# Attention stretches and the row of DMAs around the first token blocks: pairs 3 to 6 in fused stretches, with loads, casts and transposing DMAs queued earlier

## The chip, the cores and the metric

One core of one Trainium2 chip. The time of a kernel is the device time of one execution in microseconds (us); medians below are over the executions of one call on one chip. Every ratio is the mean time of one kernel's fast executions over the mean of the other's fast executions of the same rounds, with a 95% interval, so it is not quite the ratio of the medians that stand beside it. Below 1 is faster than the kernel before. "Span" is the time from the first to the last instruction of one profiled execution; it is about 1.7 us shorter than the device time.

## The reference

```python
def _attn_ref(q, k, v):                       # q, k, v: 8 x 8 x 576 x 64
    scores = scale * np.matmul(q, k.transpose(0, 1, 3, 2))
    gamma = 1.0 - 2.0 ** (-5.0 - np.arange(H, dtype=np.float32))
    Dmat = np.where(rel >= 0, gamma[:, None, None] ** rel[None, :, :], 0.0)
    return np.matmul(scores * Dmat[None], v)

def _moe_ref(x, w_a, w_b, w_out):             # x: 4608 x 512, d_ff = 1536
    return ((x @ w_a) * (x @ w_b)) @ w_out
```

A decaying (retention) attention feeds a bilinear feed-forward layer. The kernel works through the tokens in blocks. Blocks 1 and 2 have 256 tokens each, block 3 and the following ones 512. Attention is done for "pairs" of 128-token groups, one or more blocks ahead of the feed-forward work that consumes them.

## The kernel before

Each pair n goes through these stages:

- its q, k and v are loaded in fp32 by DMAs issued on SyncE (two DMAs of 256 KB per tensor);
- GpSimd (POOL) casts and scales them to bf16;
- two transposing DMAs, again on SyncE, turn q and k into qkT;
- a "half stretch" of TensorE (PE) matmuls takes the pair in: kv products for the running state, and sc, the scores, which read qkT;
- another takes it out: o from the states and from the masked scores.

A stretch may be fused: pair n in and pair n-1 out, four sets of 32 small matmuls in a row.

In the feed-forward work pa and pb are the products of x with w_a and w_b. ScalarE (ACT) copies pa to ha, VectorE (DVE) multiplies ha and pb into hT, and po is the output product, which is copied to osb and stored. In the kernel before, pa, pb and kv share the four result buffers (in PSUM) of the pool ps_ffn. The additions of kv to the running state are called "sums", and xT is the finished x of a block.

```python
    def load_pair(n):
        paired[n] = []
        for name, src in (("qf", q), ("kf", k), ("vf", v)):
            t = stage.tile([128, 2 * DM], FP32, tag=name, name=name + "2")
            for kp, r0, m, b, s0 in rows_of(n):
                nc.sync.dma_start(t[r0:r0 + m, kp * DM:(kp + 1) * DM] ..., src[...])
            paired[n].append(t)

    def turn(n):                       # the transposing DMAs, in SyncE's row too
        for w in (0, 1):
            nc.sync.dma_start_transpose(qkT[:, w]..., qkb[:, w])

    def keyed(n):                      # kv of a pair; banks of pa/pb ("ab")
        kvs = [ps_ffn.tile([128, 2, HP, 64], FP32, tag="ab", name=f"kv{a}")
               for a in (0, 1)]
        # ... 32 matmuls, then four additions on VectorE, in one piece:
        later.append(lambda: [add(i) for i in range(4)])

    def stretch(into, outof):
        flush()
        if outof is not None:
            # ... o2 tile, from_states(outof), fence copy on ScalarE
        if into is not None:
            convert, convert_swapped = keyed(into)
            masked = matched(into)     # sc <- qkT: needs the transposes landed
        if outof is not None:
            scaled = from_keys(outof, o, begun)     # o <- sT, vb
            later.append(lambda: scaled(0)); later.append(lambda: scaled(1))
        # ...

    # positions are in units of 512-column matmuls of the feed-forward work
    nc.sync.dma_start(gate, wo_sb[0:1, 3, 0:64])    # waits for output weights
    # ... loads of the last opening steps, then:
    for n in (FIRST, FIRST + 1):       # FIRST = 3
        load_pair(n)
    todo += [(178, stretch, (3, None)), (204, stretch, (None, 3)),
             (228, stretch, (4, None)), (250, stretch, (5, 4)),
             (280, stretch, (None, 5)), (304, stretch, (6, None)),
             (372, stretch, (7, 6)), (408, stretch, (8, 7))]
    casts = {3: 140, 4: 159, 5: 192, 6: 246, 7: 281, 8: 330}
    turns = {4: 196, 5: 222, 6: 258, 7: 338, 8: 345}
    loads = {5: 130, 6: 223, 7: 258.1, 8: 281.1, 9: 345.1, 10: 345.2}
```

The functions in `later` run one at a time between the feed-forward products. The tiny "gate" transfer waits for output weights to land, and SyncE's loads stand behind it, so it decides when the whole row of loads begins (in the profile before, SyncE waited 23.2 us at it for those weights, issued it at 33.45 us and the first load behind it at 34.15 us).

## Time and profile before

| what | number | where from |
|---|---|---|
| time | 333.99 us, median of 3 (333.43 to 334.01) | timing |
| span, PE busy | 332.2 us, 98% | profile |
| first matmul of blocks 1, 2, 3, 4 | 54.12, 73.43, 94.46, 129.00 us | PE timeline |
| gate transfer starts | 33.45 us | SyncE timeline |
| pair 4's transposes issued / used by PE | 67.0 and 69.2 us / 76.4 us | SyncE and PE timelines |

How to read the timelines below: start, duration, engine, line of the kernel, operation, output<-inputs, shape and how many in the group. A bracket at the end gives idle time just before the group, and what ended it.

### The profile page before, as it was taken

To read this page: it belongs to the slowest core of one execution; us is meant where nothing else is said; L and a number is where in the kernel's file an instruction comes from. 1 tells how busy PE (TensorE), PEld (TensorE's weight loads), DVE (VectorE), ACT (ScalarE), POOL (GpSimd) and SP (SyncE) were. 2 spreads that over 40 slices of the span, in tenths; PEclk is the share of its full clock that TensorE was granted. 3 is DMA by queue.
4 is the path that set the end of the run, shared out by engine and by line. 5 is a ranking of instruction groups with operands and counts; after the bars stand their busy time and mean duration, and the time that the engine had idled before them with its cause. 6 is when DMAs were issued, how large, how long until landed. Compare 5 with 4: busy or idle time off the path is not lost.

```text
span 332.2 us, 8708 instructions
## 1 busy us (share of the span) xinstructions
PE 324.9 (98%) x3648; PEld 167.7 (50%) x3648; DVE 163.6 (49%) x292; ACT 128.3 (39%) x275; POOL 114.8 (35%) x146
## 2 busy tenths in 40 slices
PE   8999999999999999999999999999999999999996
PEld 4754457857644554545454545454445444444443
DVE  5744435556646465656266625662456246414321
ACT  7734834445415344353135323532332333213321
POOL 3860078550747377446054404360430000000000
PEclk9999999999999999999999999999999999999999
DMA  7999999989999999994599257955760420031013
GB/s 212 249 186 208 259 228 231 204 163 163 176 226 235 216 201 237 230 202 95 136 229 217 51 132 176 220 87 147 170 128 4 136 56 0 2 95 34 1 26 100
DMA packets 143175, 50.37 MB, mean 152 GB/s; under 512 B 124576, under 2 KB 138656, under 8 KB 143136
## 3 DMA queue, kind: packets, MB, share of 16 engines
q1 hardware_dynamic: 138384, 45.10, 65.6%
q0 software_dynamic: 4752, 4.72, 8.8%
q8 instruction: 28, 0.46, 0.6%
q14 instruction: 11, 0.09, 0.1%
HBM read 37.75 MB, written 9.44 MB: 142 GB/s over the span
## 4 chain that ended last, share of the span: by engine, by line
PE 93%; DVE 2%; DMA 2%; ACT 1%; issue 1%; SPq 0%; POOL 0%; ACTq 0%; DVEq 0%; POOLq 0%
PE po L709 28%; PE pb L689 27%; PE pa L674 27%; PE o L594 2%; DMA qf<-in_q_dram 2%; PE o L581 2%; PE sc L555 1%; PE kv L500 1%; DVE sums L520 1%; PE kv L357 1%; PE tp L314 1%; PE sc L329 1%; PE o L407 1%; PE w L733 0%; SPq L151 0%
## 5 line engine op out<-in xcount | busy, mean ns | idle before, releaser
L694 DVE TENSOR_TENSOR hT<-ha,pb 128x512 bf16<-128x512 bf16 (+1 forms) x120 | 75.7, 633 | 97.6 <-PE pb L689 89.0
L682 ACT CAST ha<-pa 128x512 bf16<-128x512 f32 (+1 forms) x120 | 64.7, 542 | 126.5 <-PE pa L674 125.8
L689 PE MATMUL pb<-xT,wb_sb 128*128 128x512 bf16 (+1 forms) x480 | 111.9, 358 | 0.4 <-DVE sums L520 0.2
L674 PE MATMUL pa<-xT,wa_sb 128*128 128x512 bf16 (+1 forms) x474 | 110.3, 358 | 0.6 <-ACT ha L682 0.4
L709 PE MATMUL po<-wo_sb,hT 128*128 128x512 bf16 (+1 forms) x444 | 97.5, 374 | 0.0
L689 PEld LDWEIGHTS <-wb_sb 128*128 128x128 bf16 x480 | 46.5, 98 | 47.4 <-DVE sums L520 1.2
L674 PEld LDWEIGHTS <-wa_sb 128*128 128x128 bf16 x474 | 45.3, 98 | 46.4 <-issue 1.3
L709 PEld LDWEIGHTS <-hT 128*128 128x128 bf16 x444 | 42.2, 98 | 46.9
L438 POOL CAST qkb<-qf 64x1024 bf16<-64x1024 f32 x15 | 15.5, 1031 | 87.3 <-DMA qf<-in_q_dram 66.7
L720 DVE COPY osb<-po 128x512 f32<-128x512 f32 (+1 forms) x18 | 12.2, 676 | 41.7 <-PE po L709 41.7
L443 POOL TENSOR_TENSOR vb<-vf,vs 128x1024 bf16<-128x1024 f32 x15 | 28.5, 1902 | 11.4 <-DMA vf<-in_v_dram 4.6
L718 ACT COPY osb<-po 128x512 f32<-128x512 f32 (+1 forms) x19 | 10.9, 574 | 43.5 <-PE po L709 43.5
L604 DVE TENSOR_TENSOR xT<-o,qs 128x512 bf16<-128x512 f32 x30 | 19.5, 682 | 6.4 <-PE o L594 6.4
L520 DVE TENSOR_TENSOR sums<-kv,sums 128x256 f32<-128x256 f32 x46 | 19.5, 423 | 2.8 <-PE kv L500 0.8
L564 DVE TENSOR_TENSOR sT<-sc,mask 128x512 bf16<-128x512 f32 x30 | 19.5, 679 | 0.0
L442 POOL CAST qkb<-kf 64x512 bf16<-64x512 f32 x30 | 17.6, 615 | 0.8
L442 POOL CAST qkb<-qf 64x512 bf16<-64x512 f32 x30 | 17.6, 616 | 0.6
L438 POOL CAST qkb<-kf 64x1024 bf16<-64x1024 f32 x15 | 15.5, 1036 | 5.4 <-DMA kf<-in_k_dram 4.6
L524 ACT CAST states<-sums 64x512 bf16<-64x512 f32 x26 | 16.0, 617 | 0.3
L733 PE MATMUL w<-ones 128*128 128x256 bf16 (+1 forms) x36 | 8.5, 367 | 1.5 <-DVE ones L195 1.5
L297 POOL CAST qkb<-kf 128x512 bf16<-128x512 f32 x5 | 3.1, 615 | 18.9 <-DMA kf<-in_k_dram 18.9
L337 DVE TENSOR_TENSOR sT<-sc,mask_s 128x1024 bf16<-128x1024 f32 x6 | 7.3, 1221 | 2.1 <-PE sc L329 2.1
(81 smaller groups left out, 155.2 us busy)
## 6 DMA issues: line engine op xcount, KB each, us to landing
qf<-in_q_dram SPq DMA_DIRECT2D x32, 256.0 KB, 4.2
kf<-in_k_dram SPq DMA_DIRECT2D x32, 256.0 KB, 5.0
vf<-in_v_dram SPq DMA_DIRECT2D x32, 256.0 KB, 5.3
out_dram<-osb SPq DMA_DIRECT2D x25, 256.0 KB, 2.2
out_dram<-osb SPq DMA_DIRECT2D x22, 128.0 KB, 2.4
wo_sb<-in_moe_w_out_dram POOLq DMA_DIRECT2D x3, 512.0 KB, 16.7
qf<-in_q_dram SPq DMA_DIRECT2D x8, 128.0 KB, 3.3
kf<-in_k_dram SPq DMA_DIRECT2D x8, 128.0 KB, 3.4
```

The source lines that it names most:

```text
L438: nc.gpsimd.tensor_copy(qkb[0:64, w], t[0:64])
L442: nc.gpsimd.tensor_copy(to[:, :, 1 - r], fro[:, :, r])
L443: nc.gpsimd.tensor_tensor(vb.rearrange("p (k h d) -> p k h d", k=2, h=H), vf.rearrange("p (k h d) -> p k h d", k=2, h=H), vs2[:, 2 if n in ...
L520: nc.vector.tensor_tensor(sums[:, i], own, prev, op=ALU.add)
L524: nc.scalar.copy(to(half(1 - r)), fro(half(r)))
L564: nc.vector.tensor_tensor(sT[:, on].rearrange("p c k s -> p (c k) s"), sc[:, on].rearrange("p c k s -> p (c k) s"), mask3.unsqueeze(1).to_ ...
L604: nc.vector.tensor_tensor(x_of(t0, 128).rearrange("p c (a s) -> p c a s", a=2), o[:, :, :, kp].rearrange("p a c s -> p c a s"), qs[:, :, s ...
L674: nc.tensor.matmul(pa[:, 0:n], wa_sb[:, c, fs], xT[:, c], start=(c == 0), stop=(c == NC - 1))
L682: nc.scalar.copy(ha[:, 0:n], pa[:, 0:n])
L689: nc.tensor.matmul(pb[:, 0:n], wb_sb[:, c, fs], xT[:, c], start=(c == 0), stop=(c == NC - 1))
L694: nc.vector.tensor_tensor(hT[:, F, 0:n], has[F][:, 0:n], pb[:, 0:n], op=ALU.mult)
L709: nc.tensor.matmul(po[:, 0:width], hT[:, F, u * 128:(u + 1) * 128], wo_sb[:, F, cols], start=(F == 0), stop=(F == NF - 1))
```

## The change

The intent: fewer separate stretches, so that PE switches less often between attention and feed-forward work; VectorE's additions placed where they hold up no product; and pairs 4 to 6 prepared early enough to be taken in sooner.

```diff
+    SPLIT = (3, 5)
-    def load_pair(n):
+    def load_pair(n, which=(0, 1, 2)):
...
-    def keyed(n):
+    def keyed(n, alone):
-        kvs = [ps_ffn.tile([128, 2, HP, 64], FP32, tag="ab", name=f"kv{a}")
-               for a in (0, 1)]
+        if alone:
+            kv = ps_o[0].tile([128, 2, 2, HP, 64], FP32, tag="o", name="kv")
+            kvs = [kv[:, a] for a in (0, 1)]
+        else:
+            kvs = [ps_ffn.tile(... as before ...) for a in (0, 1)]
...
-        later.append(lambda: [add(i) for i in range(4)])
+        parts = [(0, 1), (2, 3)] if n in SPLIT else [(0, 1, 2, 3)]
+        for part in parts:
+            later.append(lambda part=part: [add(i) for i in part])
...
-    for n in (FIRST, FIRST + 1):
+    for n in range(FIRST, FIRST + 3):
         load_pair(n)
...
-    todo += [(178, stretch, (3, None)), (204, stretch, (None, 3)),
-             (228, stretch, (4, None)), (250, stretch, (5, 4)),
-             (280, stretch, (None, 5)), (304, stretch, (6, None)),
+    todo += [(170, stretch, (3, None)), (197, stretch, (4, 3)),
+             (246, stretch, (5, 4)), (280, stretch, (6, 5)),
              (372, stretch, (7, 6)), (408, stretch, (8, 7))]
...
-    casts = {3: 140, 4: 159, 5: 192, 6: 246, 7: 281, 8: 330}
-    turns = {4: 196, 5: 222, 6: 258, 7: 338, 8: 345}
-    loads = {5: 130, 6: 223, 7: 258.1, 8: 281.1, 9: 345.1, 10: 345.2}
+    casts = {3: 104, 4: 104.1, 5: 143, 6: 200, 7: 250, 8: 330}
+    turns = {4: 104.2, 5: 151, 6: 210, 7: 338, 8: 345}
+    loads = {7: 212, 8: 271, 9: 345.1, 10: 345.2}
+    todo += [(150, load_pair, (6, (0, 1))), (152, load_pair, (6, (2,)))]
```

More of the change, by code (lines that the diff above doesn't have):

```diff
@@ L131 @@
     paired = {}
-    def load_pair(n):
+    def load_pair(n, which=(0, 1, 2)):
         if n >= NP:
             return
-        paired[n] = []
-        for name, src in (("qf", q), ("kf", k), ("vf", v)):
+        paired.setdefault(n, [])
+        for i in which:
+            name, src = (("qf", q), ("kf", k), ("vf", v))[i]
             t = stage.tile([128, 2 * DM], FP32, tag=name, name=name + "2")
@@ L491, in keyed @@
         qkb, vb = of(natural, n)
-        kvs = [ps_ffn.tile([128, 2, HP, 64], FP32, tag="ab", name=f"kv{a}")
-               for a in (0, 1)]
+        if alone:
+            kv = ps_o[0].tile([128, 2, 2, HP, 64], FP32, tag="o", name="kv")
+            kvs = [kv[:, a] for a in (0, 1)]
+        else:
+            kvs = [ps_ffn.tile([128, 2, HP, 64], FP32, tag="ab",
+                               name=f"kv{a}") for a in (0, 1)]
         begun = Begun()
@@ L614, in stretch @@
         flush()
+        if into == FIRST:
+            ps_next("ps_pair")
         if outof is not None:
-            if outof == FIRST:
-                ps_next("ps_pair")
             o = ps_o[0].tile([128, 2, HP, 2, 64], FP32, tag="o", name="o2")
@@ L624, in stretch @@
         if into is not None:
-            convert, convert_swapped = keyed(into)
+            convert, convert_swapped = keyed(into, outof is None)
             masked = matched(into)
@@ L699, in ffn_block @@
         for u in range(n // 128):
-            rows = slice(tok0 + u * 128, tok0 + (u + 1) * 128)
-            final = rows.stop == NTOK
+            final = tok0 + (u + 1) * 128 == NTOK
             osb = o_pool.tile([128, DM], FP32, tag="osb", name="osb")
```

## The prediction

> **What bounds the kernel now.** I read the page's busy table and the chain that ended last first, then the waits of the stretch from 54 to 118 us, then the timelines of PE, DVE and SyncE there.
>
> ```profile
> PE 324.9 (98%) x3648; PEld 167.7 (50%) x3648; DVE 163.6 (49%) x292; ACT 128.3 (39%) x275; POOL 114.8 (35%) x146
> ...
> PE 93%; DVE 2%; DMA 2%; ACT 1%; issue 1%; SPq 0%; POOL 0%; ACTq 0%; DVEq 0%; POOLq 0%
> ```
>
> TensorE is busy 98% of 332.2 us and holds 93% of the chain. A change that removes no matmul (here the count stays the same: in the built order only their places differ) can win only what PE loses between matmuls. So I measured this loss where the change works: token blocks 1 and 2 (256 tokens each, 54.12 to 94.46 us) and block 3 (512 tokens, to 117.29 us). The PE timeline shows the pace and the loss:
>
> ```profile
> 62.00 0.60 PE L674 MATMUL pa<-xT,wa_sb 128*128 128x256 bf16 x4
> 62.43 0.60 PE L689 MATMUL pb<-xT,wb_sb 128*128 128x256 bf16 x4
> 62.96 0.45 PE L500 MATMUL kv<-vb,qkb 64*64 64x64 bf16 x32
> 63.24 0.46 PE L555 MATMUL sc<-qkT 64*64 64x64 bf16 x32
> 63.63 0.61 PE L674 MATMUL pa<-xT,wa_sb 128*128 128x256 bf16 x4
> 64.08 0.60 PE L689 MATMUL pb<-xT,wb_sb 128*128 128x256 bf16 x4
> 64.70 0.60 PE L674 MATMUL pa<-xT,wa_sb 128*128 128x256 bf16 x4
> 65.26 0.60 PE L689 MATMUL pb<-xT,wb_sb 128*128 128x256 bf16 x4
> 65.76 0.60 PE L674 MATMUL pa<-xT,wa_sb 128*128 128x256 bf16 x4
> 66.51 0.61 PE L689 MATMUL pb<-xT,wb_sb 128*128 128x256 bf16 x4 [0.16 <-DVE sums L520]
> ```
>
> Starts count here, since matmuls overlap. An undisturbed group of four takes 0.437 us (62.00 to 62.43). After the half stretch of pair 3 (kv and sc) six groups take 3.33 us (63.63 to 66.96) where 2.62 would do: 0.71 us lost with hardly any "idle" shown. The DVE timeline says why:
>
> ```profile
> 64.78 0.42 DVE L694 TENSOR_TENSOR hT<-ha,pb 128x256 bf16<-128x256 bf16 x1 [1.23 <-PE pb L689]
> 65.12 1.79 DVE L520 TENSOR_TENSOR sums<-kv,sums 128x256 f32<-128x256 f32 x4
> 66.83 0.41 DVE L694 TENSOR_TENSOR hT<-ha,pb 128x256 bf16<-128x256 bf16 x1
> 67.16 0.68 DVE L564 TENSOR_TENSOR sT<-sc,mask 128x512 bf16<-128x512 f32 x1
> ```
>
> Four additions hold DVE for 1.79 us, and until they end the two kv tiles keep two of the four PSUM buffers through which pa and pb rotate. PE then waits in turn for ACT (64.70) and DVE (65.26).
>
> [...]
>
> **The change part by part.** First the ideal work of blocks 1 and 2: 48 groups x 0.437 = 20.95 us, 48 output matmuls (L709) x 0.216 = 10.36, four PE transposes sets x 0.22 = 0.88: 32.2 us. The span is 40.34, so 8.1 us are attention work and loss.
>
> Attention before, each from the end of the undisturbed pace to the next big matmul: pair 3 in 0.76; pair 3 out 1.28 (it contains a wait for the fence copy); pair 4 in 0.76; pair 5 in with 4 out 1.37 (83.32 to 84.69); pair 5 out 1.25; sum 5.42. Lost pace: 0.71 + 1.27 + 0.71 = 2.69. Together 8.11, so the account closes. Block 3 adds pair 6 in (0.76) and 7 in with 6 out (1.33), 22.83 us in all, without loss.
>
> After: 3 in; 4 in with 3 out; 5 in with 4 out; 6 in with 5 out; then 7 with 6.
> - Stretches: 0.76 + 3 x 1.36 = 4.84 in blocks 1 and 2 (before 5.42), and block 3 loses its 0.76. Gain 5.42 + 0.76 - 4.84 = 1.34 us. The full stretch is cheap because its four sets of 32 small matmuls follow at 0.27 to 0.3 us and the fence copy hides behind kv and sc.
> - Pair 3's kv moves to the two o banks, which are idle then, and its sums come two at a time between hT products. All four buffers stay in rotation; DVE needs 0.34 + 0.90 us per step of 0.875, so it falls behind by about 0.4 us in each of two steps, within the slack of the freed buffers. Loss 0.71 falls to about 0.1: gain 0.6.
> - Pair 4's half stretch in block 2 goes; its sums now fall in block 1's output phase, where DVE has no hT. Gain 1.27, if the banks come free in time.
> - Pair 5's sums stay in block 2, split in two. But here kv keeps two banks until the second half is done, so pa and pb run on the other two longer: I step it through at 1.13, 1.63, 2.19, 2.80, 3.25, 3.70, 4.13 us after the stretch against 3.50 ideal: loss 0.63 against 0.71. Gain 0.1.
> - Pair 6 in with 5 out stands in block 2's output phase with only 8 output matmuls left (1.73 us) before block 3, whose first matmul reads all of x of pairs 4 and 5. In the built order DVE does four sums, half of x, the copy of the output tile, then the other half of x. Sums can begin about 0.5 us before the stretch ends and take 1.79 (+1.3); half x 0.65 (+1.95); the copy waits for the last output matmul (+1.95 to +2.6); half x to +3.25. Block 3 could begin at +1.73. So PE stands about 1.5 us. Before there were no sums between, and pa followed at once:
>
> ```profile
> 92.72 1.90 PE L709 MATMUL po<-wo_sb,hT 128*128 128x512 bf16 x8
> 94.46 1.03 PE L674 MATMUL pa<-xT,wa_sb 128*128 128x512 bf16 x4
> ```
>
> - Loads, casts, transposes: bytes are unchanged. Pair 5's loads start at about 54.2 instead of 58.5 us and take some 6.4 us, as they do before. The transposes of pair 4 are then issued at about 62.0 and 63.4 us and land 3.8 to 4.6 us later, at 66 to 68. PE reaches sc of pair 4 at about 68.6 us (54.12 + 10.5 + 0.9 + 0.9 + 1.7 + 0.6). The margin is under 1 us; I charge 0.2 us for the chance. Pair 5 lands at about 77 to 78 and is needed at 80.4; pair 6 at about 83.5 and 89. Those are hidden.
>
> ```profile
> 67.02 3.48 SPq L469 DMA_TRANSPOSE qkT<-qkb  x2
> 70.60 4.86 SPq L645 DMA_DIRECT2D out_dram<-osb  x4
> 75.56 3.45 SPq L469 DMA_TRANSPOSE qkT<-qkb  x2
> ```
>
> Here the first pair of transposes waits for its loads' queue and ends at 70.5 against a use at 76.4: the old order has 5 us to spare, the new one spends it.
>
> Sum: 1.34 + 0.6 + 1.27 + 0.1 - 1.5 - 0.2 = 1.6 us; with 334.0 us before that is 332.4. After block 3's output phase the PE order is the same as before and already without waits (117.29 to 129.00 us is all busy), so the gain should reach the end untouched.
>
> **Rivals.**
> - The wait before block 3 is absent or small (the DVE order is less tight than I step it). For: the osb copy takes only 0.69 us, and sums might start earlier. Against: the DVE order is fixed in the program, and in a later stretch of the same form sums and x take 3.07 us together. It would give 330.9.
> - Transposes of pair 4 land late, and PE stands at the sc of that stretch with block 2 behind it. For: DMA is saturated there (1.06 busy share from 54 to 94 us), transposes took up to 5.1 us to land, and the margin is small. It would cost 1 to 2 us: 333.4 to 334.4.
> - DVE falls behind in block 1 and the stretch of 3 in still stalls, and the sums of pair 5 hold banks longer. For: six large DVE operations in five steps. It would cost 0.5 to 1 us: about 333.
> - No gain at all: what is saved before 94 us is waited for afterwards by late casts of pairs 7 and 8. Against: those transposes are not used before block 3's second half, and POOL is idle for 12.5 us waiting for kv before.
>
> **Range and chances.** 332.4, from the sum. All rivals lie between 330.9 and 334.4, and run-to-run spread before is 0.6 us, so 330.7 to 334.0 should hold it 8 times in 10. Two per cent are 6.7 us; blocks 1 and 2 hold only 8.1 us of attention and loss altogether, so neither side is likely: faster 0.02, same 0.96, slower 0.02.
>
> **What would show it.** PE busy must stay near 324.9 us while the span falls. In the PE timeline: two stretches fewer; the pace after pair 3's half stretch near 0.437; an idle of about 1.5 us on PE before block 3's first pa, put down to DVE xT; three or four slow groups after pair 5's stretch. On SyncE, transposes of pair 4 issued at about 62 to 64 us. If the sc of pair 4 shows a wait for a DMA, the second rival holds. If block 3 starts within 0.5 us of its ideal, my reading of the DVE order is wrong. If the time moves by over 4 us, the account of 8.1 us misses something.

## The result and the profile after

The changed kernel took 333.75 us (333.55 to 334.06, 4 executions), the kernel before 333.77 us beside it (333.43 to 334.01, 4 executions): ratio 1.0001 [0.9984, 1.0018]. There is no gain where 1.6 us was forecast. The profiled span is 331.8 us, clock 1.0.

The waits of PE in the changed kernel (waiting for, from whom: total us, times, longest). The lines "issue" of 0.2 us are mostly single matmuls missing from the record (3,612 matmuls are in it beside 3,648 weight loads):

```profile
PE po L716 <- issue: 1.6, 10, 0.2
PE w L740 <- DVE ones L197: 1.5, 1, 1.5
PE pa L682 <- DVE xT L612: 1.4, 1, 1.4
PE sc L563 <- DMA qkT<-qkb: 1.3, 1, 1.3
```

The wait at w is the start of the program and was there before. The other two are new: pa of block 3 waits for VectorE (forecast), and sc waits for transposing DMAs for 1.3 us. The line below answers to the "PE 93%" line of the prediction, with DMA up from 2% to 5%. This is no measure of lost time: 5% of the span is over 16 us, and the chain counts a transfer on it from its issue (pair 4's second transpose stands in it with 4.02 us from 66.07, the moment of its issue). It shows only that the last chain now runs through more DMAs:

```profile
PE 86%; DMA 5%; SPq 2%; issue 2%; DVE 2%; ACT 1%; POOL 1%; DVEq 0%; POOLq 0%; ACTq 0%
```

The PE timeline of the changed kernel at the half stretch of pair 3, and at the fused stretch of pair 4 in, 3 out:

```profile
61.54 0.44 PE L563 MATMUL sc<-qkT 64*64 64x64 bf16 x32
61.91 0.61 PE L682 MATMUL pa<-xT,wa_sb 128*128 128x256 bf16 x4
...
66.29 1.89 PE L716 MATMUL po<-wo_sb,hT 128*128 128x512 bf16 x7
68.11 0.45 PE L589 MATMUL o<-qkT,states 64*64 64x64 bf16 x32
68.38 0.44 PE L506 MATMUL kv<-vb,qkb 64*64 64x64 bf16 x32
70.14 0.45 PE L563 MATMUL sc<-qkT 64*64 64x64 bf16 x32 [1.32 <-DMA qkT<-qkb]
```

From 61.91 to 66.29 us are ten groups in 4.38 us, 0.438 each: the lost pace of 0.71 us behind pair 3 is gone. But at 68.82 us PE is ready for sc of pair 4 and stands until 70.14. SyncE's timeline says what came before the transposes:

```profile
55.20 2.29 SPq L142 DMA_DIRECT2D qf<-in_q_dram  x2
57.59 3.38 SPq L142 DMA_DIRECT2D kf<-in_k_dram  x2
61.07 1.87 SPq L142 DMA_DIRECT2D vf<-in_v_dram  x2
63.04 1.46 SPq L653 DMA_DIRECT2D out_dram<-osb  x2
64.60 3.28 SPq L471 DMA_TRANSPOSE qkT<-qkb  x2
```

These are pair 5's six loads, two stores, and then pair 4's transposes. The same loads in the kernel before, and the stores behind them:

```profile
58.53 2.10 SPq L140 DMA_DIRECT2D qf<-in_q_dram  x2
60.73 1.99 SPq L140 DMA_DIRECT2D kf<-in_k_dram  x2
62.81 2.27 SPq L140 DMA_DIRECT2D vf<-in_v_dram  x2
65.18 1.74 SPq L645 DMA_DIRECT2D out_dram<-osb  x2
```

The loads take 7.84 us (55.20 to 63.04); in the kernel before they took 6.65 (58.53 to 65.18). The casts that the transposes read are not what is late: POOL had ended those of pair 4 at 59.36 us. I put the delay down to the DMA engines, whose mean busy share is 1.16 from 54 to 64 us, against 1.04 before, at about the same rate (216 and 225 GB/s). The second transpose is issued at 66.07 us and lands at 70.10 us, 0.04 us before PE goes on.

The forecast wait in front of block 3, on VectorE:

```profile
91.66 1.34 DVE L526 TENSOR_TENSOR sums<-kv,sums 128x256 f32<-128x256 f32 x3
92.92 0.68 DVE L612 TENSOR_TENSOR xT<-o,qs 128x512 bf16<-128x512 f32 x1
93.53 0.69 DVE L727 COPY osb<-po 128x512 f32<-128x512 f32 x1
94.14 0.68 DVE L612 TENSOR_TENSOR xT<-o,qs 128x512 bf16<-128x512 f32 x1
```

Sums, half of x, the output copy, the other half of x: the order that the prediction stepped through. Block 3's first pa starts at 94.88 us, after 1.38 us of idle time.

### The profile page after: what moved, and what is told of

The parts are those of the page before. It is cut to its first block, busy times and chain, and to the rows that moved or that the text cites. A ratio compares the mean times of both kernels' runs of the same rounds, so it can differ in the third digit from the quotient of the medians.

```text
span 331.8 us, 8671 instructions
## 1 busy us (share of the span) xinstructions
PE 319.8 (96%) x3612; PEld 168.1 (51%) x3648; DVE 163.7 (49%) x292; ACT 128.6 (39%) x275; POOL 114.6 (35%) x146
## 4 chain that ended last, share of the span: by engine, by line
PE 86%; DMA 5%; SPq 2%; issue 2%; DVE 2%; ACT 1%; POOL 1%; DVEq 0%; POOLq 0%; ACTq 0%
PE po L716 27%; PE pb L697 27%; PE pa L682 26%; SPq L153 2%; DMA vf<-in_v_dram 2%; DMA qf<-in_q_dram 2%; PE o L589 2%; PE o L602 1%; DMA qkT<-qkb 1%; PE sc L563 1%; PE kv L506 1%; PE kv L359 1%; DVE sums L526 0%; POOL qkb L440 0%; PE pa L664 0%
## 5 line engine op out<-in xcount | busy, mean ns | idle before, releaser
L682 PE MATMUL pa<-xT,wa_sb 128*128 128x512 bf16 (+1 forms) x459 | 108.4, 357 | 2.8 <-DVE xT L612 1.4
L716 PE MATMUL po<-wo_sb,hT 128*128 128x512 bf16 (+1 forms) x430 | 95.0, 373 | 1.8 <-issue 1.6
L563 PE MATMUL sc<-qkT 64*64 64x64 bf16 x480 | 7.4, 195 | 1.3 <-DMA qkT<-qkb 1.3
```

The costliest lines, as they stand in the source:

```text
L682: nc.tensor.matmul(pa[:, 0:n], wa_sb[:, c, fs], xT[:, c], start=(c == 0), stop=(c == NC - 1))
L716: nc.tensor.matmul(po[:, 0:width], hT[:, F, u * 128:(u + 1) * 128], wo_sb[:, F, cols], start=(F == 0), stop=(F == NF - 1))
```

## The experiments

First theory (A): the forecast sum is right except for the transposes of pair 4, which land later than charged, because they stand behind a DMA-bound row (mean busy share of the DMA engines 1.16 from 54 to 64 us). Rivals: the lost time lies in PE's longer stretches; or the missing gain is the spread of one measurement. Sixteen runs were made, in four calls of four, each call on another chip and each with its own runs of the kernel before. The second call had no run of the changed kernel.

A caution on the ratios: eight executions that count as fast had a granted clock of 0.993 to 0.995 and took 335.02 to 338.22 us. They are one each of the kernel before in calls one, three and four, and of g_after, u, b3, c and b4. "At full clock" below means without them. The ratios are given as they stand, and where it matters the ratio at full clock stands beside.

### First call: the changed kernel again, and its two waits taken away

**a_again**: the changed kernel, unedited.

> The changed kernel unaltered, as the control of this call and a second look at its waits. Theory A (the fused stretches and the free buffers did save about 3.3 us, and two new waits of TensorE gave it back: 1.32 us at the sc matmuls of pair 4 for its transposes, 1.38 us at block 3's first pa for DVE's xT): both waits are there again, and the time is that of before within 0.3%. Rival C (the wait for the transposes came only from weights that landed late in the one profiled execution, 34.89 us instead of 33.44 us): SyncE starts its row of loads near 33.5 us this time, the wait at sc of pair 4 is under 0.4 us, and the span is about 1 us shorter than before. Rival B (fused stretches save nothing): waits or not, the time stays at that of before.

Measured: 332.54 us against 334.16, ratio 0.9949 [0.9908, 0.999]. The same file that won nothing is here 1.6 us faster by the medians; at full clock the ratio is 0.9961, 1.3 us. Its row of loads began at 33.3 us and not 34.9, and pair 4's second transpose landed at 69.07 us and not 70.10:

```profile
69.12 0.45 PE L563 MATMUL sc<-qkT 64*64 64x64 bf16 x32 [0.61 <-DMA qkT<-qkb]
```

So the result of one call is not the whole truth about this change. The wait is there in both profiles, half as long here, and what happens to the row moves the time.

**e1_turn_before_stores**: pair 4's transposes ahead of the two stores.

```diff
-    casts = {3: 104, 4: 104.1, 5: 143, ...
-    turns = {4: 104.2, 5: 151, ...
+    casts = {3: 103, 4: 103.1, 5: 143, ...
+    turns = {4: 103.2, 5: 151, ...
```

> The changed kernel with one thing moved: pair 4's transposes stand ahead of the first two stores of block 0 in SyncE's row instead of behind them. Theory A: they are issued about 1.5 us sooner and land at about 68.6 us, so the wait at sc of pair 4 falls from 1.32 to 0 to 0.4 us. The rest of the row is as long as it was, so pair 5's transposes still land at about 81.4 us, which TensorE now reaches at about 80.5 us: a wait of 0.5 to 1 us may appear at sc of pair 5. Time 0.1 to 0.4% below that of before. Rival B: the wait goes and the time doesn't move. Rival C: no wait to remove, no change against the control.

Measured: 333.20 us, ratio 0.9962 [0.9926, 0.9999]. The wait at sc of pair 4 is gone, but pair 5's sc, whose transposes landed at 81.32 us, now waits 0.66 us. Taking time from one place of the row gave it to the next. By the medians the edit is 0.7 us slower than the control beside it; in the profiles 0.27 us of that is a later start of block 1 and 0.25 us a stop of the kind shown under e2.

**e2_earlier_6_5**: the stretch of pairs 6 and 5 earlier, so that twelve output matmuls and not eight lie between it and block 3.

```diff
-             (246, stretch, (5, 4)), (280, stretch, (6, 5)),
+             (246, stretch, (5, 4)), (276, stretch, (6, 5)),
```

> The changed kernel with one number changed: the stretch that takes pair 6 in and pair 5 out stands four output matmuls earlier (at the end of the first output tile of block 2), so that 12 instead of 8 output matmuls lie between it and block 3, and DVE does both halves of xT before the copy of the output tile. Theory A: xT is ready about 2.55 us after the stretch, the 12 matmuls take 2.6 us, and the wait of 1.38 us before block 3 falls to 0 to 0.2 us; time 0.4% below that of before (about 332.4 us where before has 333.8). Rival B or C: the wait before block 3 may go, but the time stays within 0.1% of the control.

Measured: 332.16 us, ratio 0.9931 [0.9895, 0.9967]. The wait for xT is gone entirely, and the wait at sc of pair 4 stays, at 0.59 us. Two stalls named "issue" appeared, of 0.34 and 0.48 us, which had been in no forecast. The first of them:

```profile
89.38 0.44 PE L602 MATMUL o<-sT,vb 64*64 64x64 bf16 x29
90.17 0.22 PE L602 MATMUL o<-sT,vb 64*64 64x64 bf16 x3 [0.34 <-issue]
90.32 2.76 PE L716 MATMUL po<-wo_sb,hT 128*128 128x512 bf16 x12
92.92 1.03 PE L682 MATMUL pa<-xT,wa_sb 128*128 128x512 bf16 x4
```

PE stops three matmuls before the end of a set, where no tile changes hands. I call stops of this kind the second loss.

**e3_both**: both edits.

> Both moves in the changed kernel. Theory A: their gains add up, less a wait of up to 1 us that may appear at sc of pair 5: 1.7 to 2.7 us below before, 331.1 to 332.1 us where before has 333.8, ratio 0.992 to 0.995. Rival B: the time of before. Rival C: only the part of the second move, 1.4 us below the control.

Measured: 332.67 us, ratio 0.9951 [0.9914, 0.9988]; no better than e2 alone. Here the gate transfer started at 35.8 us, and all three of pairs 4, 5 and 6 waited at sc (0.61, 0.63 and 0.30 us). The row, starting 2.5 us later than in the first control, is not ready, and for pair 6 PE arrives earlier, since its stretch stands four units earlier.

### Second call: the row delayed and relieved

**n_after_no_stores**: the stores of block 0 left out, a wrong result.

```diff
-                store(tok0 // 128 + u, cols, osb)
+                if tb:
+                    store(tok0 // 128 + u, cols, osb)
```

> Changed kernel with the eight half-block stores of block 0 left out (1 MB less in SyncE's row between the loads and the transposing DMAs; wrong result on purpose, rows of block 0 stay unwritten). Theory A, the row of loads, stores and transposes is what takes the gain away: the transposes of pair 4 issue at least 2 us earlier, both waits of PE at sc for qkT vanish (below 0.1 us in sum), the wait of block 3 for xT stays at about 1.4 us, and the time is 0.5 to 1.5 us below the changed kernel's in the same run, near 331.8 us. It no longer matters whether the weights land early or late. Rival B, PE's own pace in the longer stretches takes it: no wait vanishes or its time comes back as gaps inside the stretches, and the time stays within 0.3 us of the changed kernel's 332.5 to 333.7.

Measured: 332.42 us, ratio 0.9954 [0.9942, 0.9967]. The expectation missed: the second transpose was issued at 64.52 us, only 0.55 us earlier than in the control of the first call, and 0.54 us of wait at sc of pair 4 remained. Only two of the eight stores lie ahead of these transposes; the loads do the rest. This run could not tell the theories apart.

**g_after_gate_late** and **g_before_gate_late**: the gate transfer waits for the second chunk of output weights, in the changed kernel and in the kernel before.

```diff
-    nc.sync.dma_start(gate, wo_sb[0:1, 3, 0:64])
+    nc.sync.dma_start(gate, wo_sb[0:1, 7, 0:64])
```

> Changed kernel whose tiny gate transfer waits for the second chunk of the output weights instead of the first, so that SyncE's whole row of loads starts about 2.5 us later and nothing else is touched. Theory A (the changed kernel has no slack at pair 4's transposes, so a late row is paid nearly one for one): the wait at sc of pair 4 grows from 0.6 to 1.3 us to 2.5 to 3.8 us and the time to 334.5 to 336 us, slower than before. Rival B (the wait is a coincidence of one run): the row catches up, the time stays at 332.5 to 333.7 us.

> The kernel before with the same later gate. Theory A: its transposes of pair 4 land about 5 us before they are used, so 2.5 us later costs nothing at sc; time within 0.4 us of the kernel before, unless the loads of the last opening steps are now late, which the changed kernel would pay as well: then the difference of the two counts. Rival B (a late row costs both alike): slower by 1 to 2.5 us.

Measured: the changed kernel goes to 334.69 us, ratio 1.0031 [1.0007, 1.0055], slower than before; the kernel before stays at 334.31 us, ratio 1.0013 [0.9998, 1.0029]. By the medians this is the direction of theory A, but the times do not show it: one of the six executions (337.05 us) had a clock of 0.995, and at full clock the ratio is 1.0007, no higher than those of two of the three controls in other calls (1.0001 and 0.9998). In the trace, which is of the fastest execution (333.25 us), the direction is there and the size was overestimated. The gate was 2.5 us later than in the first control (35.76 against 33.26 us), but the transposes only 1.0 us (64.53 against 63.52), and the wait was 1.35 us and not 2.5 to 3.8: where SyncE started later, it issued its loads faster for a while.

**u_unfused_6_5**: the stretch of pairs 6 and 5 taken apart.

```diff
-             (246, stretch, (5, 4)), (280, stretch, (6, 5)),
+             (246, stretch, (5, 4)), (280, stretch, (None, 5)),
+             (304, stretch, (6, None)),
```

> Changed kernel with the stretch of pairs 6 and 5 taken apart again: output half of pair 5 at its place, key half of pair 6 later, inside block 3. Theory A: the wait of block 3 for xT falls from 1.38 us to below 0.3, the fused stretch's saving of about 0.65 to 0.75 us (one half stretch's switch and lost pace) is given back in block 3: 0.5 to 0.9 us faster than the changed kernel, so 331.7 to 333.0 us. Rival B: DVE is late anyway and the wait stays above 1 us: 0.5 us slower than the changed kernel.

Measured: 332.84 us, ratio 0.9967 [0.9942, 0.9992]. The wait for xT vanished. Six executions lay between 331.83 and 335.02 us, too wide for a difference of half a microsecond (the highest had a clock of 0.995), so for the time this is inconclusive. Pair 4 still waits 0.56 us at sc. Its trace shows that the VectorE wait is the price of fusing this one stretch, as forecast.

### Third call: a reordered row

**a_third**: the changed kernel, unedited.

> The changed kernel once more, as the control of this call. Theory A (its gain is the forecast one less what PE waits at sc for the transposes, and that wait follows how late the weights land): 332.3 to 333.7 us, the single executions in two groups about 1 us apart, the profiled one with 0.5 to 0.7 us of wait at sc of pair 4 if its gate transfer starts near 33.3 us, and 1.3 us if it starts near 34.9 us. Rival (no gain at all, the 332.5 us of the earlier control was luck): all near the kernel before.

Measured: 334.11 us (333.11 to 334.67), ratio 0.9992 [0.9963, 1.002]. The expectation, that an early gate means a short wait, failed: the gate started at 33.35 us, as early as in the first control, but the wait at sc of pair 4 was 1.13 us. The second transpose was issued at 66.76 us, 1.7 us after that of the first control, because single issues in the row took longer: 3.30 against 2.17 us for pair 4's k loads, 2.36 against 1.45 us for the first transpose. How late the weights land is then only one of the things that move the row. PE also lost 0.54 us by the second loss, in front of an output product at 123.98 us.

**b1_row_reordered**: like e2, with the v load of pair 5 behind pair 4's transposes, and pair 5's transposes ahead of pair 6's k load.

```diff
-    for n in range(FIRST, FIRST + 3):
+    for n in range(FIRST, FIRST + 2):
         load_pair(n)
+    load_pair(FIRST + 2, (0, 1))
...
-             (246, stretch, (5, 4)), (280, stretch, (6, 5)),
+             (246, stretch, (5, 4)), (276, stretch, (6, 5)),
...
-    todo += [(150, load_pair, (6, (0, 1))), (152, load_pair, (6, (2,)))]
+    todo += [(104.3, load_pair, (5, (2,))), (150, load_pair, (6, (0,))),
+             (151.5, load_pair, (6, (1,))), (152, load_pair, (6, (2,)))]
```

> Changed kernel with the stretch of pairs 6 and 5 four units earlier, the v load of pair 5 moved behind pair 4's transposes, and pair 5's transposes put between pair 6's q and k loads: nothing but order in the row of DMAs and one place on PE. Theory A: pair 4's transposes start about 2 us earlier (near 62 us), both waits at sc and the wait for xT are gone (below 0.2 us in sum), time 331.3 to 332.0 us, and the executions no longer in two groups. Rival (the time comes back elsewhere, as a wait for vb of pair 5 or for pair 6's transposes): 332.2 us or more, with such a wait in the trace.

Measured: 331.63 us, ratio 0.9917 [0.9888, 0.9947], the fastest: 0.8% below the kernel before, 0.7% at full clock (0.9926). Its fast executions (330.92 to 332.12 us) lie clear of the control's (333.11 to 334.67), and the profiled spans differ by 2.43 us (332.36 and 329.93), where the waits and stops that are gone come to 2.41. The wait for xT is gone, and pair 4 waits 0.16 us although the gate was late (35.26 us). The claim of no wait at sc failed: pair 6 waits 0.63 us. I put this down to its k load, which was moved back; b4 below shows that this is not all of it.

```profile
PE sc L563 <- DMA qkT<-qkb: 0.8, 2, 0.6
```

**b2_row_reordered_gate_late**: b1 with the later gate.

> The reordered row with the later gate transfer (start of the whole row 2.5 us later). Theory A: with about 1.5 to 2 us of slack won, the later row costs at most 0.7 us against the reordered row with the early gate, where it cost the changed kernel about 2 us. Rival (the later gate harms by something other than pair 4's transposes, such as the opening's last loads): it costs 1.5 to 2.5 us here too, with no wait at sc in the trace.

Measured: 332.44 us, ratio 0.9952 [0.9916, 0.9989], 0.8 us over b1. Pairs 4 and 5 have no wait; pair 6 waits 2.07 us. The two gates differ little in the profiled executions (35.26 and 35.65 us), so what of the 0.8 us belongs to the gate stays open. The trace shows where a delay would be paid: at pair 6, which has no slack.

**b3_row_reordered_kv_back**: b1 with two parts of the change undone.

```diff
-    SPLIT = (3, 5)
+    SPLIT = ()
-            convert, convert_swapped = keyed(into, outof is None)
+            convert, convert_swapped = keyed(into, False)
```

> The reordered row with two parts of the change undone: kv of a half stretch again in the banks of the projections, and the additions of pairs 3 and 5 in one piece. Theory A (the sum of the prediction): after the half stretch of pair 3 the first product waits for DVE and PE loses about 0.7 us of pace again, after (5,4) at most 0.2 us more: 0.5 to 0.9 us slower than the reordered row. Rival (these parts are worth nothing): within 0.3 us of it.

Measured: 333.01 us, ratio 0.9973 [0.9931, 1.0014], 1.4 us over b1. Behind the half stretch of pair 3 ten groups that take 4.38 us in b1 take 5.62 us:

```profile
64.86 0.61 PE L697 MATMUL pb<-xT,wb_sb 128*128 128x256 bf16 x4 [0.16 <-DVE sums L526]
...
67.59 1.89 PE L716 MATMUL po<-wo_sb,hT 128*128 128x512 bf16 x8 [0.38 <-ACT ha L690]
```

So these two parts work. In the new order they are worth 1.24 us at this place; the kernel before lost 0.71 us there, of which 0.6 was to be won. The rest of the difference is no clean measure: b3 had no wait at sc and 0.94 us of the second loss.

### Fourth call: is the row all of it?

**a_fourth**: the changed kernel, unedited.

> The changed kernel as the control of this call. Theory A: 332.5 to 334.2 us, with 0.5 to 1.4 us of wait at sc of pair 4 in its profile; its span is that of the kernel before less 1.8 us plus this wait, within 0.5 us. Rival B (something else takes the gain): that account misses by over 0.7 us.

Measured: 334.33 us, ratio 0.9989 [0.9956, 1.0021]. PE waits 1.61 us at sc of pair 4 and 0.38 at that of pair 5. The profile puts the first to another engine:

```profile
70.41 0.45 PE L563 MATMUL sc<-qkT 64*64 64x64 bf16 x32 [1.61 <-DVE sums L526]
```

But the transpose landed at 70.36 us, and in the other controls too PE went on 0.04 to 0.05 us after the landing. A name in the bracket is only the last event that the profile saw.

**c_after_v5_later**: only the v load of pair 5 moved (the first and last hunk of b1, with pair 6's loads as they were).

> Changed kernel with the v load of pair 5 alone moved behind pair 4's transposes (two transfers of the row). Theory A: the transposes of pair 4 start about 1.5 to 2 us earlier, the wait at sc of pair 4 falls below 0.2 us, the wait for xT before block 3 stays at about 1.4 us, pair 5's wait at sc stays below 0.7 us: 0.4 to 1.2 us faster than the control of the same call. Rival B: no faster than the control by over 0.3 us.

Measured: 333.78 us (332.01 to 335.29), ratio 0.9971 [0.9932, 1.0009]. The mechanism came as expected: the transposes of pair 4 start at 62.04 us, 2.4 us before the control's, its wait is gone, pair 5 waits 0.40 us, xT 1.38 us. By the medians it is 0.5 us faster than the control, with intervals that overlap. The time did not follow in the profiled execution. In block 3, after the stretch of pairs 8 and 7:

```profile
122.04 0.47 PE L602 MATMUL o<-sT,vb 64*64 64x64 bf16 x32
123.92 2.33 PE L716 MATMUL po<-wo_sb,hT 128*128 128x512 bf16 x10 [1.42 <-issue]
```

**n2_no_stores_v5_later**: c with the stores of block 0 left out too (wrong result).

> As before, and the eight half-block stores of block 0 left out (wrong result on purpose), so that the row is relieved ahead of both pairs' transposes, on the changed kernel's own order of PE. Theory A: no wait at sc for qkT of pairs 4 to 6 at all (below 0.1 us), xT 1.4 us; time that of the kernel before less 1.8 us within 0.4: 331.8 to 332.6 us, single executions within 0.6 us of each other. Rival B (longer stretches lose it elsewhere): above 332.8 us without a wait at sc.

Measured: 333.13 us (332.31 to 333.80), ratio 0.9948 [0.9911, 0.9985]; 1.2 us below the control by the medians, and no execution is above the control's fastest (333.80 to 334.82). So of the edits that leave PE's order alone this one shows in the times that the waits at sc cost something (though it also stores less). No wait at sc is left, but the span of 331.9 us has again the second loss:

```profile
68.53 0.44 PE L506 MATMUL kv<-vb,qkb 64*64 64x64 bf16 x32
68.85 0.45 PE L563 MATMUL sc<-qkT 64*64 64x64 bf16 x32
```

```profile
PE pa L682 <- DVE xT L612: 1.4, 1, 1.4
PE po L716 <- issue: 1.1, 1, 1.1
```

The rival's condition, a time over 332.8 us without a wait at sc, is met. So theory A alone does not hold: something else takes part of the gain. It is not the longer stretches themselves (in this trace sc of pair 4 follows kv after 0.32 us and no other idle time over 0.25 us is left in blocks 1 and 2), but a stop after a stretch.

**b4_only_v5_later**: e2 with the v load of pair 5 moved, without b1's swap.

> Stretch of pairs 6 and 5 four units earlier and the v load of pair 5 moved, without the swap of pair 6's k load that the reordered row also had. Theory A: the 0.6 us wait at sc of pair 6 that the swap caused is gone, pair 5's transposes come about 1.7 us later and may cost up to 0.4 us: 331.2 to 332.0 us, within 0.4 us of the reordered row or better. Rival: pair 5's wait exceeds 0.7 us and the time 332.2.

Measured: 332.84 us (331.37 to 335.97), ratio 0.9953 [0.9907, 0.9999]. Pair 4 has no wait, pair 5 0.24 us; but pair 6 still waits 0.61 us, so the swap was not the only reason for that. Its second transpose was issued at 84.90 us and landed at 89.88. Whether it is slower than b1 cannot be said: they ran in different calls and its executions spread over 4.6 us.

### What the second loss is

The traces of all 18 runs (the first two and these 16) say much about it without a further kernel. The page counts the packets on the instruction queue:

```profile
q8 instruction: 28, 0.46, 0.6%
```

They are 28 packets of 16,384 bytes, and the built program has 7,318 instructions for PE. No trace states how many of these a packet holds, nor that this queue carries PE's. My estimate is 256, from the two stops in e2: they stand at instructions 2,498 and 3,266 of the built order, 768 apart, and 9 and 12 packets had arrived at them, so three packets stand for 768 instructions. The count fits: 7,318 / 256 is 28.6. A fused stretch is 128 weight loads and 128 matmuls, so by this estimate it uses up one packet in 1.25 us (122.56 to 123.81 us in the kernel before).

- Place: in e2 and in b3 PE stopped before the last three matmuls of the same set, at instruction 2,498 of the built order; in c, n2, e1, e2, the third and fourth controls before the output product after the stretch of pairs 8 and 7, at instruction 3,266. These are 9 x 256 + 194 and 12 x 256 + 194: by the estimate the same place in a packet, and at the stops just 9 and 12 packets had arrived. In none of the 18 traces did the weight load at place n x 256 + 194 start less than 1.19 us after the arrival of packet n, for any n from 1 to 27.
- Time: each stop at the second place ended 1.19 to 1.55 us after a packet of that queue had arrived (in c it arrived at 122.48 us and PE went on at 123.92).
- When: six of the 18 traces have a stop of over 0.2 us at the second place, and they are just the six in which the packet came later than 0.6 us before sc of pair 8 started. In the kernel before it came 1.42 us ahead of it. With the stops at the first place it is seven traces, and stops of 0.25 to 1.42 us.

I conclude that PE waited for its own instructions. Place, time and condition agree, but no kernel was made to move a packet's boundary, so this is read from traces and not tested. Why the packet was late in some executions is not shown.

## Why the prediction was wrong

It forecast a gain of 1.6 us. Four calls of the changed kernel gave ratios of 1.0001, 0.9949, 0.9992 and 0.9989; their mean, 0.9983, is a gain of 0.6 us. At full clock they are 1.0001, 0.9961, 1.0001 and 0.9998, a gain of 0.3 us. What each step came to:

- Pair 3 in without lost pace: right. Ten groups in 4.38 us: all of the 0.71 us won, where 0.6 was forecast. Undoing it (with pair 5's split) lost 1.24 us at this place.
- Pair 5's split sums: right. After (5,4), groups end after 4.11 us against 3.50 ideal, loss 0.61, forecast 0.63. SPLIT leaves the four additions whole and puts other work between them, and no run tests it alone.
- VectorE in front of block 3: right. 1.38 us, forecast about 1.5; e2 and u removed it as the reading of the order says.
- **Failed step: "The transposes of pair 4 are then issued at about 62.0 and 63.4 us" and "The margin is under 1 us; I charge 0.2 us for the chance."** In four profiles the second was issued at 65.07 to 66.76 us, and PE waited 0.61 to 1.61 us at sc of pair 4, each time. The term mis-sized was pair 5's six loads, "some 6.4 us, as they do before": they took 7.84, 7.94, 8.10 and 8.25 us. (6.4 is the sum of the three durations in the kernel before; with the gaps it was 6.65 there.) In the first profile they also began 1.0 us later than forecast, at 55.20 us. PE came about when it was expected: 68.82 us, where the prediction's own terms add to 68.7 and not 68.6. The old row had stores between the loads and the new one has eighteen loads of pairs in a row, on DMA engines whose mean busy share is 1.16. The rival "transposes of pair 4 land late" described this, with 333.4 to 334.4 us; it was charged with only 0.2 us. A margin that depends on a row with this busy share should have been charged as a wait.
- The same step failed for pair 5: "Pair 5 lands at about 77 to 78" and "Those are hidden". It landed at 80.32 to 82.62 us in the four profiles. That PE waited there only 0 to 0.38 us was luck: the wait at pair 4 had held PE back, and in e1, which removed that wait, pair 5 cost 0.66 us.
- Two readings behind this step were too kind. "Ends at 70.5" is the end of an issue and not a landing: in g_before, with the row a little later, pair 4's second transpose landed 3.3 us after its issue, at 73.33, for a use at 76.43, so the old order had some 3 us to spare and not 5. And of the 5.5 us in which SyncE waited for casts at its transposes (eight waits), the longest piece, 2.0 us at 67.02, names a cast of pair 5 (64.37 to 68.96 us), while pair 4's had ended at 58.46; at 86.54 us the wait is real (the cast ended at 86.51).
- A step that the prediction did not have: "After block 3's output phase the PE order is the same as before and already without waits", so the gain "should reach the end untouched". It did not always. The second loss took 0.54 and 0.25 us in two of the four controls, and up to 1.42 us in c.

With these two terms the sum closes. Take the span of the kernel before, 332.20 us, less 1.81 us (the forecast gain without the 0.2 us charged), plus the measured waits at sc, plus the stops for instructions, plus the shift of block 1's start against 54.12 us:

| kernel | waits at sc | stops | shift | sum | span measured |
|---|---|---|---|---|---|
| changed, first profile | 1.32 | 0 | 0.05 | 331.76 | 331.85 |
| a_again | 0.61 | 0 | -0.27 | 330.74 | 330.88 |
| a_third | 1.28 | 0.54 | 0.02 | 332.23 | 332.36 |
| a_fourth | 1.99 | 0.25 | 0.02 | 332.66 | 332.78 |
| e1 | 0.66 | 0.25 | 0 | 331.31 | 331.49 |
| g_after | 1.35 | 0 | -0.30 | 331.44 | 331.54 |
| n_after | 0.54 | 0 | -0.44 | 330.48 | 330.65 |
| c | 0.40 | 1.42 | 0 | 332.20 | 332.32 |
| n2 | 0 | 1.09 | 0.20 | 331.68 | 331.91 |

All nine miss by 0.09 to 0.23 us, on the same side. For the reordered kernels e2, e3, b1, b2 and b4 the same sum, less the 1.38 us for xT that is gone there, misses by -0.09 to 0.43 us. So the forecast sum of 1.81 us was right as a sum within about 0.2 us, PE's longer stretches can have cost no more than that beyond it, and the missing time lies in the waits at sc and the stops. It does not show each of its terms: at pair 3's place 0.71 us were won and not 0.6, so others must have been too large. And it is an account of single profiled executions. In the times, n2 and b1 lie clear of their controls and e1 and c do not.

Open: why the row ran about a microsecond earlier in the first control than in the three other profiles; how much of this is the chip and how much each execution; and what delays the instruction packets.

## What to carry to other kernels

Read slack from a row of DMAs as busy as this one (mean busy share 1.16 from 54 to 64 us) as if each transfer took its time at the measured rate, and take the transfers from the order that the row will have, not from the old one; here a margin under a microsecond became a wait in all four profiles. Pair 4's second transpose landed 3.1 to 4.4 us after its issue in them, and a 256 KB load 4.4 to 5.3 us (medians in c). Three reorderings of this row handed the lateness to a later user (0.66 us at pair 5 in e1, 0.63 and 0.61 us at pair 6 in b1 and b4), so look at which of them has slack. And a small change needs its control on more than one chip: one call said 0.5% faster and three said nothing. Look at the clock of each execution too: one slow execution of the kernel before made up 0.1% of that 0.5%.
